# Step one of a Fourier convolution in four 64 by 64 tiles, with kv and the two intermediates stored in another order

## The chip, the cores and the metric

The kernel runs on one core of a Trainium2 chip. The metric is the device time of one execution in microseconds. The five engines of the core have short names here: PE (TensorE matmul, with PEld for its weight loads), DVE (VectorE), ACT (ScalarE), POOL (GpSimd) and SP (SyncE, whose queue issues most DMAs).

## The reference

The inputs are 2048 tokens by 640 channels in float32.

```python
def _A_ref(q, k, v, shift_k, ssm_k, ssm_D):          # per channel
    k_shift = sum over t<4 of k_pad[:, t:t+S] * shift_k[:, 3-t]
    kv = k_shift * v
    y = irfft(rfft(pad(kv, 2S)) * rfft(pad(ssm_k, 2S)))[:S] + kv * ssm_D
    return q * y

def _B_ref(x, w1, b1, w2, b2):                       # MLP over the tokens, F = 1728
    u = gelu(layernorm(x)^T @ w1 + b1)
    return (u @ w2 + b2)^T

sa, ca, ga, sb, cb, gb = split(silu(c) @ w_mod)
x = q
h = layernorm(x) * (1 + ca) + sa
x = x + ga * _A_ref(h, k, v, shift_k, ssm_k, ssm_D)
h = layernorm(x) * (1 + cb) + sb
x = x + gb * _B_ref(h, w1, b1, w2, b2)
```

## The kernel before

The first 350 us of the execution are the long convolution, the rest is the token MLP. The change lies in the first part alone.

The convolution goes through the channels in five chunks of 128 (`NC`, the loop `for c in range(NC)`). Within a chunk the causal convolution of length 2048 is done as a Fourier transform of size 64 by 32 on TensorE. A token index is split into n1 (64 values, on the partitions) and n2 (32 values, free), a frequency into k1 (64) and k2 (32). The two halves of 64 channels of a chunk lie on the lower and the upper 64 partitions (h). A channel within the half is a pair member c or e (2) and an index i (32).

The stages of a chunk, with their names and lines in the profile:

- kv (`kv_ops`, all on L59): four taps multiplied and added, then times v, written into X. DVE does it, but for one of the four groups of the first two chunks, which POOL does. X holds n2 outside and the 64 channels inside. The kv of the next chunk is spread between DVE's other work by `fill` and `dv`, and each group's end issues the loads of a later chunk on SP.
- `perm` (L159): ACT copies the filter from KSR into P in the order (i, n2, e).
- `step1` (L212, evacuation L214): the transform over n1. Side 0 is kv, side 1 the filter. A side has four tiles t of eight indices i. For each i, two matmuls (real and imaginary part, ri) take the data as weights (128 partitions by 64) and the constant F1 as moving operand with 128 columns, block diagonal over the two halves h. Each result occupies 64 partitions and 128 columns of a two-bank PSUM tile, and ACT copies a tile of 1024 elements to Z.
- `f2` (L227): the transform over n2, eight groups g of eight k1. W2 is the weights, Z is the moving operand, 64 columns: both sides, with the 32 indices. ACT copies the filter's spectrum out (L231), DVE multiplies twice into P (L59, `mul`), and POOL adds into Y (L59, `add`; DVE in the last chunk). P has two halves, used in turn.
- `i2` (L256, evacuation L259): the inverse over k2, from Y into T2 in two rounds r, on 32-row tiles. Each round takes two PSUM tiles and four evacuations of 512 elements.
- `i1` (L272): the inverse over k1, in two halves, on tiles of 64 rows and 64 columns: V1 is the weights and T2 the moving operand. Then `gate` multiplies on DVE and adds on POOL.

Z occupies `T_z`, 8192 elements of each partition, side 0 in the lower 4096 and side 1 in the upper 4096. T2 lies over side 1's half. The order of the work is written out by hand: in a chunk c come f2 of c, step one on side 0 of chunk c+1, i2 and i1 of c, and step one on side 1 of c+1. In chunk 0, parts of the modulation (`mod_part`, L343) stand between the tiles of side 0, and the loads of the next w_mod parts, of later k and v and of V1 follow on SP. PSUM tiles come from a ring of three (`psum()`), in turn for all of these stages.

The lines that matter most of what the change rewrites:

```python
Z = T_z.rearrange("p (s t a k e) -> p s t a k e", s=2, t=4, a=8, e=2)
T2 = T_z[:, 4096:8192].rearrange("p (a m e) -> p a m e", a=32, e=2)
```

## Time and profile before

| | |
|---|---|
| median of 3 runs | 771.51 us (770.37 to 774.67) |
| the profiled execution's own time | 767.61 us |
| its span | 765.8 us |
| mean granted TensorE clock | 0.935 |
| PE busy | 665.1 us (87%) |
| DVE busy | 507.1 us (66%) |
| ACT busy | 292.2 us (38%) |
| POOL busy | 177.8 us (23%), all in the first half |

A group row of the profile reads: line, engine, operation, output from input by the program's names, shapes and count, then busy time in us and mean duration of one in ns, then the idle time of the engine just before these instructions and what ended it. Busy times of PE are counted once where matmuls run at the same time on different tiles of the array, while the mean duration is that of one instruction from start to end. So busy time over count tells how often one is finished, and the mean does not. A row of the timeline reads: start, length, engine, line, what it does and how many instructions are merged in it, and in brackets the idle time before it with its releaser. The `L59` lines are the helper through which all tensor-tensor operations go.

### The profile page before, as it was taken

The page shows a single profiled execution, that of the slowest core. Times are in us where ns is not written, and L with a number is a line of the kernel's source. Part 1 is how long each engine was busy: PE and PEld are TensorE (multiplying, and loading weights), DVE is VectorE, ACT ScalarE, POOL GpSimd, SP SyncE. Part 2 cuts the span into 40 slices and gives each one's busy share as a digit, 9 for nine tenths or more (in the row PEclk, how much of TensorE's full clock was granted, in tenths as well). Part 3 has the DMA queues.
Part 4 walks back from the last instruction along what each step waited for, and adds up shares of the span by engine and source line. Part 5 has one row for each costly group of instructions (what it writes and reads, how often), then busy time and mean ns, then how long its engine had stood idle before and what let it go on. Part 6 is the DMA issues. An engine that isn't in the chain of part 4 may idle for free.

```text
span 765.8 us, 20747 instructions
## 1 busy us (share of the span) xinstructions
PE 665.1 (87%) x9117; PEld 641.5 (84%) x9117; DVE 507.1 (66%) x883; ACT 292.2 (38%) x424; POOL 177.8 (23%) x173
## 2 busy tenths in 40 slices
PE   0597948698997989974599999999999989999997
PEld 0597747597997989863599999999999989999997
DVE  4668569974874853958899331312358958888887
ACT  0342324334534544643566622312224323332322
POOL 2268013732842832903253000000000000000000
PEclk9999969888988988976689999999999999999999
DMA  9988886216215024395000244253334262555420
GB/s 169 268 219 250 223 209 140 63 44 119 71 30 112 5 57 135 130 219 111 2 1 1 56 89 77 56 105 61 81 110 141 66 183 86 157 165 156 118 84 35
DMA packets 172425, 84.26 MB, mean 110 GB/s; under 512 B 88959, under 2 KB 164910, under 8 KB 172334
## 3 DMA queue, kind: packets, MB, share of 16 engines
q1 hardware_dynamic: 168110, 81.88, 43.3%
q10 hardware_dynamic: 4224, 1.05, 0.8%
q8 instruction: 71, 1.16, 0.6%
q14 instruction: 20, 0.16, 0.1%
HBM read 72.43 MB, written 10.49 MB: 108 GB/s over the span
## 4 chain that ended last, share of the span: by engine, by line
PE 57%; DVE 20%; DMA 5%; ACT 5%; issue 4%; POOL 4%; SPq 3%; ACTq 0%; DVEq 0%; POOLq 0%
PE pst L420 25%; PE pst L227 8%; PE pst L212 8%; PE pst L909 6%; DVE m_w L59 4%; PE pst L272 4%; PE pst L256 4%; DVE m_x L59 3%; POOL y L59 2%; ACT m_w L822 2%; DVE sm L519 2%; PE pst L834 2%; DMA p<-in_B_w_dram 1%; ACT z L259 1%; DVE m_v L59 1%
## 5 line engine op out<-in xcount | busy, mean ns | idle before, releaser
L59 POOL TENSOR_TENSOR y<-p 128x256 f32<-128x256 f32 x78 | 103.0, 1404 | 37.2 <-DVE p L59 37.2
L227 PE MATMUL pst<-z,w 128*64 128x64 f32 x2560 | 96.3, 240 | 7.2 <-ACT z L214 6.1
L227 PEld LDWEIGHTS pst<-z,w 128*64 128x64 f32 x2560 | 94.9, 141 | 9.1 <-ACT z L214 7.3
L420 PE MATMUL pst<-r_z,wb 128*128 128x320 f32 x504 | 82.8, 321 | 16.1 <-ACT r_z L653 10.6
L420 PEld LDWEIGHTS pst<-r_z,wb 128*128 128x128 f32 x504 | 79.1, 198 | 18.0 <-ACT r_z L653 11.8
L214 ACT ACTIVATE z<-pst 128x1024 f32<-128x1024 f32 x40 | 46.4, 1159 | 69.5 <-PE pst L212 69.5
L59 DVE TENSOR_TENSOR p<-pst,kt 128x512 f32<-128x512 f32 x80 | 52.3, 691 | 30.4 <-ACT kt L231 24.3
L256 PEld LDWEIGHTS pst<-v,y 32*128 32x128 f32 x1280 | 46.1, 220 | 7.6 <-ACT z L259 4.6
L256 PE MATMUL pst<-v,y 32*128 32x64 f32 x1280 | 48.0, 307 | 4.7 <-ACT z L259 4.0
L420 PE MATMUL pst<-h_x,wb 128*128 128x320 f32 x336 | 51.1, 309 | 0.0
L420 PEld LDWEIGHTS pst<-h_x,wb 128*128 128x128 f32 x336 | 49.7, 188 | 0.0
L212 PEld LDWEIGHTS pst<-v,x 128*64 128x64 f32 x640 | 44.7, 219 | 5.7 <-POOL y L59 3.0
L212 PE MATMUL pst<-v,x 128*64 128x128 f32 x640 | 45.8, 309 | 3.4 <-DVE x L59 3.4
L231 ACT ACTIVATE kt<-pst 128x512 f32<-128x512 f32 x40 | 25.1, 628 | 55.1 <-PE pst L227 27.3
L834 PE MATMUL pst<-r_z,m_w 128*128 128x320 f32 x222 | 42.8, 312 | 2.0 <-DVE m_w L59 1.4
L59 DVE TENSOR_TENSOR wb<-x,wb 128x1024 fp32r<-128x1024 f32 (+1 forms) x32 | 36.8, 1188 | 11.4 <-ACT wb L409 11.3
L272 PEld LDWEIGHTS pst<-z,v 64*64 64x64 f32 x1280 | 28.8, 186 | 18.1 <-ACT z L259 9.8
L272 PE MATMUL pst<-z,v 64*64 64x64 f32 x1280 | 29.7, 270 | 16.0 <-ACT z L259 8.6
L714 ACT ACTIVATE pst<-pst,sm 128x640 f32<-128x640 f32 x14 | 10.7, 767 | 85.9 <-PE pst L420 85.9
L212 PE MATMUL pst<-v,p 128*64 128x128 f32 x640 | 36.2, 273 | 4.1 <-ACT p L159 1.9
L212 PEld LDWEIGHTS pst<-v,p 128*64 128x64 f32 x640 | 35.0, 137 | 4.6 <-ACT p L159 2.1
L420 PE MATMUL pst<-h_a,wb 128*128 128x320 f32 x252 | 38.8, 309 | 0.0
(209 smaller groups left out, 1281.8 us busy)
## 6 DMA issues: line engine op xcount, KB each, us to landing
x<-in_B_w_dram SPq DMA_DIRECT2D x24, 512.0 KB
m_v<-in_B_w_dram SPq DMA_DIRECT2D x15, 384.0 KB
x<-in_B_w_dram SPq DMA_DIRECT2D x14, 384.0 KB
in<-in_A_k_dram SPq DMA_DIRECT2D x40, 128.0 KB
aux<-in_A_ssm_k_dram SPq DMA_DIRECT2D x10, 512.0 KB
m_x<-xs SPq DMA_DIRECT2D x28, 160.0 KB
out_dram<-m_x SPq DMA_DIRECT2D x28, 160.0 KB
w<-in_const_w_dram SPq DMA_DIRECT2D x2, 2048.0 KB
```

What stands on the lines that cost most here:

```text
L59: TT = lambda eng, o, a, b, op: eng.tensor_tensor(o, a, b, op=op)
L212: pe.matmul(ps[64 * ri:64 * ri + 64, o:o + 128], lhs, F1[:, 128 * ri:128 * ri + 128], start=True, stop=True)
L214: act.activation(Z[:, side, t].rearrange("p a k e -> p e a k"), ps.rearrange("p (e a k) -> p e a k", a=8, e=2), AF.Copy)
L227: pe.matmul(ps[64 * h:64 * h + 64, o:o + 64], W2[k1 // 32][:, 2 * (k1 % 32) + ri], rhs, start=True, stop=True)
L231: act.activation(kt.rearrange("p (m i) -> p m i", i=32), pv[:, :, 1], AF.Copy)
L256: pe.matmul(pp[qd // 2][:, o:o + 64], Y[p, ri, i:i + 2].rearrange("p i k -> p (i k)"), V2[p, 64 * ri:64 * ri + 64], start=ri == 0, stop=ri ...
L272: pe.matmul(ps[64 * b:64 * b + 64, 512 * e + 64 * jj:512 * e + 64 * jj + 64], V1[p, ri, n2], T2[p, :, 32 * ri + n2], start=ri == 0, stop=r ...
L420: pe.matmul(ps[0:m, h, 0:320], w_.bitcast(F32R), r_[:, 320 * h:320 * h + 320].bitcast(F32R), start=first and i == 0, stop=last and i == 2)
L519: dve.bn_stats(bst[:, j, h, :], XR(j, 320 * h, 320))
L822: act.activation(W[n][0].bitcast(F32R), a(w_), AF.Copy)
L834: pe.matmul(bank[n], w[:, i].bitcast(F32R), r.bitcast(F32R), start=i == 0 and k == 0, stop=i == 6 and k == 2)
L909: pe.matmul(acc[s][:, h, 0:320], w[:, f_].bitcast(F32R), u[r + h].bitcast(F32R), start=f_ == 0 and k == 0, stop=f_ == NF - 1 and k == 2)
```

## The change

Four things change, and no arithmetic does.

X gets the order of P, (i, n2, c): the last operation of `kv_ops` writes it through `XP`, so that a weight of side 0 lies in a row of 64 elements, and that write steps 64 elements (256 bytes) between successive elements.

Step one runs the two halves h as matmuls of their own: 64 rows, 64 weight columns, 64 moving columns. The four of an index i (h and ri) lie on the four quadrants of the array, and the two h write to different PSUM banks. The number of matmuls doubles from 16 to 32 a tile.

Z becomes (s, k1, h, i): the evacuation writes with a step of 64 elements, and f2's moving operand becomes two runs of 32 successive elements, where it was 32 pairs, 256 elements apart. The last tile of side 1 is evacuated in two instructions, k1 below 32 first. f2's groups 0 to 3 read only k1 below 32.

T2 becomes (m, s), with the 64 values of s in a row: i2's evacuations write with a step of 64 elements, and i1's moving operand is one run of 64, where it was 32 pairs.

The order of the instructions on each engine stays as it was, apart from the doubled matmuls and the split evacuations. The waits of f2's groups are drawn from the new regions.

```diff
-    KSP = P.rearrange("p (i m) -> p i m", i=32)
+    KSP, XP = [t.rearrange("p (i m) -> p i m", i=32) for t in (P, X)]
...
-    Z = T_z.rearrange("p (s t a k e) -> p s t a k e", s=2, t=4, a=8, e=2)
-    T2 = T_z[:, 4096:8192].rearrange("p (a m e) -> p a m e", a=32, e=2)
+    Z = T_z.rearrange("p (s k h i) -> p s k h i", s=2, k=64, h=2)
+    T2 = T_z[:, 4096:8192].rearrange("p (m s) -> p m s", m=64)
...
-        ops.append(lambda: TT(eng, X.rearrange("p (n i) -> p n i", i=64)[:, 8 * g:8 * g + 8], S_,
-                              VX[:, 8 * g:8 * g + 8], ALU.mult))
+        two = lambda t: t.rearrange("p n (c i) -> p n c i", c=2)
+        ops.append(lambda: TT(eng, XP.rearrange("p i (n c) -> p n c i", c=2)[:, 8 * g:8 * g + 8], two(S_),
+                              two(VX[:, 8 * g:8 * g + 8]), ALU.mult))
...
-            lhs = KSP[:, i] if side else X.rearrange("p (m i) -> p i m", i=32)[:, i]
-            o = 512 * (a % 2) + 128 * (a // 2)
-            for ri in range(2):
-                pe.matmul(ps[64 * ri:64 * ri + 64, o:o + 128], lhs, F1[:, 128 * ri:128 * ri + 128], start=True,
-                          stop=True)
-        act.activation(Z[:, side, t].rearrange("p a k e -> p e a k"),
-                       ps.rearrange("p (e a k) -> p e a k", a=8, e=2), AF.Copy)
+            for h in range(2):
+                r = slice(64 * h, 64 * h + 64)
+                for ri in range(2):
+                    pe.matmul(ps[64 * ri:64 * ri + 64, 512 * h + 64 * a:512 * h + 64 * a + 64],
+                              (KSP if side else XP)[r, i], F1[r, 128 * ri + 64 * h:128 * ri + 64 * h + 64], start=True,
+                              stop=True)
+        n = 32 if side and t == 3 else 64
+        for k in range(0, 64, n):
+            act.activation(Z[:, side, k:k + n, :, 8 * t:8 * t + 8].rearrange("p k h i -> p h i k"),
+                           ps.rearrange("p (h a k) -> p h a k", h=2, a=8)[:, :, :, k:k + n], AF.Copy)
...
-                    rhs = bass.AP(tensor=T_z.tensor, offset=T_z.offset + 128 * h + 2 * k1,
-                                  ap=[T_z.ap[0], [256, 32], [1, 2]])
+                    rhs = bass.AP(tensor=T_z.tensor, offset=T_z.offset + 64 * k1 + 32 * h,
+                                  ap=[T_z.ap[0], [4096, 2], [1, 32]])
...
-            act.activation(T2[:, 8 * qd + 4 * r:8 * qd + 4 * r + 4].rearrange("p a m e -> p a e m"),
-                           pp[qd // 2][:, 512 * (qd % 2):512 * (qd % 2) + 512].rearrange("p (a e m) -> p a e m",
-                                                                                         a=4, e=2), AF.Copy)
+            act.activation(T2[:, :, 16 * qd + 8 * r:16 * qd + 8 * r + 8].rearrange("p m s -> p s m"),
+                           pp[qd // 2][:, 512 * (qd % 2):512 * (qd % 2) + 512].rearrange("p (s m) -> p s m", s=8),
+                           AF.Copy)
...
-                                  V1[p, ri, n2], T2[p, :, 32 * ri + n2], start=ri == 0, stop=ri == 1)
+                                  V1[p, ri, n2], T2[p, 32 * ri + n2], start=ri == 0, stop=ri == 1)
```

## The prediction

> **What bounds the kernel now.** I read the page first (span, chain), then the groups kept apart by shape, then the timeline and the table by stage of the first 350 us, where every edit lies.
>
> ```profile
> span 765.8 us, 20747 instructions
> PE 57%; DVE 20%; DMA 5%; ACT 5%; issue 4%; POOL 4%; SPq 3%; ACTq 0%; DVEq 0%; POOLq 0%
> PE pst L420 25%; PE pst L227 8%; PE pst L212 8%; PE pst L909 6%; DVE m_w L59 4%; PE pst L272 4%; PE pst L256 4%; DVE m_x L59 3%; POOL y L59 2%; ACT m_w L822 2%; DVE sm L519 2%; PE pst L834 2%; DMA p<-in_B_w_dram 1%; ACT z L259 1%; DVE m_v L59 1%
> ```
>
> The chain gives step one (L212) 8% of the span, about 61 us, and ACT's evacuations a little over 1%. The sizes behind it (busy total, mean of one, then idle before):
>
> ```profile
> L227 PE MATMUL pst<-z,w 128*64 128x64 f32 x2560 | 96.3, 240 | 7.2 <-ACT z L214 6.1 <-DVE p L59 1.1
> L212 PE MATMUL pst<-v,x 128*64 128x128 f32 x640 | 45.8, 309 | 3.4 <-DVE x L59 3.4
> L212 PE MATMUL pst<-v,p 128*64 128x128 f32 x640 | 36.2, 273 | 4.1 <-ACT p L159 1.9 <-DVE aux L59 1.8 <-issue 0.4
> L272 PE MATMUL pst<-z,v 64*64 64x64 f32 x1280 | 29.7, 270 | 16.0 <-ACT z L259 8.6 <-DMA v<-in_const_v_dram 5.3 <-issue 2.1
> L214 ACT ACTIVATE z<-pst 128x1024 f32<-128x1024 f32 x40 | 46.4, 1159 | 69.5 <-PE pst L212 69.5
> L259 ACT ACTIVATE z<-pst 128x512 f32<-128x512 f32 x40 | 21.4, 629 | 32.9 <-PE pst L256 32.9
> L159 ACT ACTIVATE p<-aux 128x2048 f32<-128x2048 f32 x5 | 10.5, 2097 | 26.0 <-POOL aux L59 26.0
> L409 ACT ACTIVATE wb<-x 128x1024 fp32r<-128x1024 f32 x24 | 24.1, 1050 | 4.7 <-PE pst L420 4.3 <-DMA x<-in_B_w_dram 0.3
> L59 POOL TENSOR_TENSOR y<-p 128x256 f32<-128x256 f32 x78 | 103.0, 1404 | 37.2 <-DVE p L59 37.2
> L59 POOL TENSOR_TENSOR t<-t 128x512 f32<-128x512 f32 x6 | 7.8, 1303 | 0.5
> ```
>
> ACT waits for PE in step one (69.5 us over 40 evacuations): a tile takes PE longer than ACT. The record counts are twice those of the code (16 matmuls a tile, 20 tiles a side, 640 records), so a matmul of step one has two records. Stage by stage (start:end and length; PE, PEld, DVE, ACT, POOL busy with counts; granted clock; DMA share, GB/s):
>
> ```profile
> 239.10:246.20 7.10, 7.10 (x129) 6.90 (x128) 5.35 (x8) 3.39 (x3) 2.38 (x1) 1.00 0.81 157
> 267.10:275.20 8.10, 8.10 (x130) 7.98 (x130) 7.85 (x4) 4.53 (x6) 7.17 (x7) 1.00 0.01 2
> 106.90:110.60 3.70, 3.69 (x136) 3.70 (x137) 1.41 (x5) 0.00 (x0) 0.00 (x0) 0.50 1.20 185
> 111.10:113.30 2.20, 2.20 (x120) 2.08 (x119) 2.13 (x6) 0.16 (x1) 0.97 (x3) 0.87 0.11 18
> 223.60:230.00 6.40, 6.40 (x124) 6.21 (x124) 1.98 (x3) 1.29 (x3) 0.00 (x0) 0.56 0.01 3
> 280.20:285.00 4.80, 4.80 (x124) 4.80 (x124) 0.00 (x0) 0.96 (x2) 0.00 (x0) 0.72 0.38 66
> ```
>
> Row one is step one on the filter (side 1), row two on kv (side 0), both at full clock: 7.1 and 8.1 us for four tiles, 1.78 and 2.03 each. The matmuls are the same; what differs is that X is read as weights in steps of 128 bytes and P in a row. The next two rows are i1, whose matmuls have exactly the new shape (64 rows, 64 columns, N of 64, the same order of the four quadrants). The last two are i2.
>
> **Step one on PE.** i1 took 54 ns a matmul at clock 0.50 (3.69 us over 136 records, two each) and 37 ns at 0.87. Times the clock that is 27 to 32 ns at full speed. A tile becomes 32 such matmuls, 0.9 to 1.0 us; I take 1.02. ACT's evacuation (1.16) then sets the pace, if it keeps that time. What of this reaches the end must be seen in each chunk:
>
> ```profile
> 239.04 7.21 PE L212 MATMUL pst<-v,p 128*64 128x128 f32 x128
> 246.35 1.07 ACT L214 ACTIVATE z<-pst 128x1024 f32<-128x1024 f32 x1 [0.64 <-PE pst L212]
> 247.47 3.77 PE L227 MATMUL pst<-z,w 128*64 128x64 f32 x95 [1.23 <-ACT z L214]
> 153.15 9.41 PE L212 MATMUL pst<-v,x 128*64 128x128 f32 x128
> 152.60 4.19 POOL L59 TENSOR_TENSOR y<-p 128x256 f32<-128x256 f32 x2 [1.17 <-DVE p L59]
> 162.49 4.01 PE L256 MATMUL pst<-v,y 32*128 32x64 f32 x132
> 210.25 8.37 PE L212 MATMUL pst<-v,x 128*64 128x128 f32 x128
> 214.78 3.22 POOL L59 TENSOR_TENSOR y<-p 128x256 f32<-128x256 f32 x1
> 218.55 4.01 PE L256 MATMUL pst<-v,y 32*128 32x64 f32 x132
> 251.60 20.38 POOL L59 TENSOR_TENSOR y<-p 128x256 f32<-128x256 f32 x16 [8.69 <-DVE p L59]
> 267.02 8.25 PE L212 MATMUL pst<-v,x 128*64 128x128 f32 x128 [0.50 <-DVE x L59]
> 275.19 4.01 PE L256 MATMUL pst<-v,y 32*128 32x64 f32 x132
> ```
>
> *Side 1, chunks 1 to 3.* Now 8.43 us from the first matmul to f2 (239.04 to 247.47), and f2 waits for the last evacuation. New: first tile 1.02, 0.1 to signal, three evacuations of 1.15, then only the first half of the last (k1 below 32, 512 elements: 0.63 as L259's), 5.2 in all. Saved 3.2 each, 9.6. The second half runs beside f2's first group.
>
> *Side 0.* i2 follows, and needs two things besides PE: all of Y from POOL, and the second and third tile evacuated, since the ring has three buffers. Chunk 1: evacuations end at 153.15 + 1.2 (9.41 for 8.37 there, a slower clock) + 0.1 + 3 x 1.16 = 157.9, POOL at 156.8; i2 starts at 158.0 for 162.5, 4.5 saved. Chunk 2: POOL ends at 218.0 whatever PE does, so only 0.5 of 8.4 us is saved; POOL's Y is the late one there. Chunk 3: ACT 271.6, POOL 272.0, i2 at 272.1 for 275.2, 3.1 saved. Chunk 4 has no side 0.
>
> ```profile
> 55.38 5.48 POOL L59 TENSOR_TENSOR y<-p 128x256 f32<-128x256 f32 x4
> 78.00 4.28 PE L212 MATMUL pst<-v,x 128*64 128x128 f32 x64
> 106.91 3.91 PE L272 MATMUL pst<-z,v 64*64 64x64 f32 x136 [5.30 <-DMA v<-in_const_v_dram]
> 151.98 1.24 PE L165 MATMUL tap<-rows 2*128 2x256 f32 x2 [5.91 <-DVE x L59]
> ```
>
> *Start and chunk 0.* f2 may start sooner, but Y starts on POOL at 55.4, after POOL's share of kv that its loads hold back: nothing saved. Tiles 2 and 3 of the side 0 at 78.0 stand ahead of the second modulation part, whose end frees the loads behind it on SP, and V1's load last of all, for which i1 waits 5.30 us: 4.28 becomes 2.2, saved 2.1 (0 to 2.5). Side 1 of chunk 0 is worth nothing: chunk 1's f2 ends on DVE (taps wait 5.91 for it).
>
> Together 9.6 + 4.5 + 0.5 + 3.1 + 2.1 = 19.8 us.
>
> **What it costs.** *PE's idle time.* i2's second half runs right after a wait of 1.0 us, at 0.56 in chunk 2 (6.40 us) and at 0.72 in chunk 3 (4.80). In the new chunk 2 PE waits some 3.5 us for POOL ahead of i2: 1.6 lost (0 if the clock holds). *Instructions.* Step one's double, and L272 stood 2.1 us by "issue" in 1280 records; 1280 more, half of them on the path: 1.0 (0 to 2).
>
> *Contiguous moving operand in f2 and i1.* f2 takes 37.6 ns a record (96.3 over 2560). The side-1 step streams 128 columns in 56.6 (36.2 over 640), so 28 would be the floor for 64: up to 0.6 us a group. Only chunk 4's f2 has no POOL or DVE pacing it; at most 4.9 us there, and 1.8 from earlier first groups. i1 reads in the same pairs and is near its floor, so I take 0.
>
> *The strided writes* are the unknown. ACT now writes Z and T2 with 256 bytes between successive elements, DVE and POOL write X so. No row shows a write that steps more than 8 bytes; that one, L159, costs nothing (2097 for 2048 elements against 1050 for 1024). Reads with a long step are slow:
>
> ```profile
> L59 DVE TENSOR_TENSOR y<-p x2: 601/816/1032, 323.2 to 324.2; 128x256 f32<-128x256 f32 x2
> L59 DVE TENSOR_TENSOR x<-tap,in x18: 676/691/702, 15.2 to 266.2; 128x512 f32<-128x512 f32 x18
> L59 DVE TENSOR_TENSOR wb<-x,wb x32: 1082/1219/1227, 324.7 to 602.7; 128x1024 fp32r<-128x1024 f32 x24, 128x896 fp32r<-128x896 f32 x8
> ```
>
> In a row DVE takes 1.03 ns a result and 0.16 us fixed (1219 less 691 over 512). With a 256-byte step in both inputs, at best 601 for 256: 1.71 a result, 0.86 a read. One access each 0.86 ns is what ACT needs at its 1.02 (1047 over 1024), so I take nothing extra for one write per element. The other end adds the full 0.86 per element: 2.04 us for 1024 elements, 1.07 for 512; 0.44 on each X write of DVE; on POOL 2.74 ns a stepped read (1404 over 512) for 1.27 (1303 over 1024), 0.75 an X write. A gain below today's cost I exclude: today's writes step 8 bytes and cost nothing.
>
> [...]
>
> **Sum.** 19.8 less 1.6 and 1.0 is 17.2. The profiled execution took 767.6 (2 outside the span) and becomes 750.4; the median of the three runs, 771.5, stands 3.9 above it, so 754.3, say 754.
>
> **Rivals.** *Strided writes at the far end (slower).* The place is ACT behind i2:
>
> ```profile
> 223.56 6.43 PE L256 MATMUL pst<-v,y 32*128 32x64 f32 x124 [1.00 <-ACT z L259]
> 231.82 5.11 PE L272 MATMUL pst<-z,v 64*64 64x64 f32 x249 [1.82 <-ACT z L259]
> ```
>
> PE waits for two evacuations in the middle and four at the end; 0.44 each is 2.6 a chunk, 10.5 in chunks 1 to 4 and 1.8 in chunk 0. Step one, bound by evacuations of 2.04, keeps 0.1 x 3 on side 1, and 1.9, 0.5, 0.9 and 1.0 on side 0. Chunk 1's four X writes add 1.8, POOL's 0.8. With clock and issue: 12.3 + 2.6 + 2.6 - 4.6 = 12.9 slower, 784. It decides at 0.49 ns an element, an evacuation of 1.66 us. For it: stepped reads do cost. Against: ACT is the slower consumer. *Between:* 1.45 us an evacuation, 0.3 an element, gives back 35% of the 30 us between the ends: 765.
>
> *PE's gaps take the clock down.* With ACT pacing, PE idles in every tile. If each of seven stages is followed by 1.6 of slow clock, 11.2 instead of 1.6 is lost: 764. Against it: f2 runs at 1.00 after a wait of 1.23 today. [...]
>
> That the four tiles don't overlap, so step one gains nothing, the i1 rows speak against; I give it nothing.
>
> **The numbers.** Forecast 0.52; strided writes slow 0.26 (768 to 785); between 0.12; clock 0.10. The low end is 19.8 + 4.9 + 1.8 saved and nothing lost: 745.0, say 744. The high end takes in most of the slow case: 780. The likeliest case's own range is 744 to 760. Half a per cent, 3.9 us, is what a measurement here tells from no change. Faster: 0.52, 0.08 of the clock's and 0.07 of the between case, 0.67. Same: 0.02, 0.05 and 0.04 of the slow case, 0.11. Slower: 0.22.
>
> **What would show it.** Right: L214 at 1.10 to 1.25 us for 1024 elements and L259 near 0.63; L212 some 1.0 us a tile with ACT no longer idle behind it; side 1 to f2 in 5.2; i2 of chunk 2 waiting for POOL. Wrong: L214 above 1.66; PEclk under 0.8 in f2; L212 above 1.5 a tile.

## The result and the profile after

The changed kernel takes 780.7 us (778.4 to 782.8) beside 771.0 for the kernel before, measured with it. The ratio is 1.0115 (1.0067 to 1.0163): slower by over 0.5%, and outside the range of 744 to 780 by 0.7 us. The profiled execution took 782.3 us.

The page of the changed kernel, its span, its granted clock in 40 slices and its chain:

```profile
span 780.5 us, 23315 instructions
PEclk9989867878966886987589999999999999999999
PE 49%; DVE 22%; DMA 8%; issue 8%; ACT 7%; SPq 5%; POOL 0%; ACTq 0%; DVEq 0%
```

PE's share of the chain falls by 8 points, and "issue" and ACT rise from 4 and 5% to 8 and 7. The groups of the first 400 us, kept apart by shape, show three things of different sign:

```profile
L217 ACT ACTIVATE z<-pst 128x1024 f32<-128x1024 f32 x35 | 65.6, 1981 | 54.5 <-PE pst L212 54.5
L262 ACT ACTIVATE z<-pst 128x512 f32<-128x512 f32 x40 | 36.4, 1057 | 30.3 <-PE pst L259 30.3
L59 DVE TENSOR_TENSOR x<-tap,in 128x512 f32<-128x512 f32 x18 | 18.9, 1051 | 2.0 <-PE pst L212 1.5
L212 PE MATMUL pst<-v,x 64*64 64x64 f32 x1280 | 31.3, 277 | 8.6 <-issue 4.7 <-DVE x L59 3.7
L212 PE MATMUL pst<-v,p 64*64 64x64 f32 x1280 | 26.7, 249 | 22.7 <-issue 17.5 <-DVE aux L59 3.6 <-ACT p L158 1.6
L230 PE MATMUL pst<-z,w 128*64 128x64 f32 x2560 | 84.3, 231 | 13.1 <-ACT z L217 6.0 <-DVE p L59 4.8 <-issue 2.2
L59 POOL TENSOR_TENSOR y<-p 128x256 f32<-128x256 f32 x78 | 90.0, 1197 | 51.9 <-DVE p L59 51.9
```

The stepped evacuations cost 0.80 to 0.84 ns an element more (1159 to 1981 for 1024, 629 to 1057 for 512). Step one's matmuls take less of PE (45.8 to 31.3 and 36.2 to 26.7 us busy, part of it at a lower clock), but on side 1 PE now stands 17.5 us for "issue" where it stood 0.4. And f2 takes 12 us less of PE (96.3 to 84.3) and POOL's Y 0.21 us less each (1404 to 1197), for which the forecast took nothing.

The timeline of PE behind chunk 1's inverse shows 6.3 of the 17.5 us:

```profile
177.91 5.34 PE L275 MATMUL pst<-z,v 64*64 64x64 f32 x256 [3.29 <-ACT z L262]
184.95 2.09 PE L212 MATMUL pst<-v,p 64*64 64x64 f32 x127 [1.70 <-issue]
189.47 2.09 PE L212 MATMUL pst<-v,p 64*64 64x64 f32 x128 [2.43 <-issue]
193.74 0.21 PE L212 MATMUL pst<-v,p 64*64 64x64 f32 x1 [2.19 <-issue]
195.13 13.02 PE L230 MATMUL pst<-z,w 128*64 128x64 f32 x384 [1.17 <-ACT z L217]
```

Side 1 is executed in pieces of 127 or 128 records, each 2.09 us long, which start 4.3 to 4.5 us apart. Every matmul record has a weight load beside it, so a piece is 256 instructions. i1 (256 records, 512 instructions) ran just before. The pages list the transfers of instructions by queue, before and after:

```profile
q8 instruction: 71, 1.16, 0.6%
q8 instruction: 81, 1.33, 0.7%
```

The ten transfers more, of 16 KB each, go with 2568 instructions more (20747 and 23315), so one brings some 257, about the 256 of a piece. In the trace of the changed kernel such a transfer lands 1.2 to 1.6 us before the end of every pause for "issue" on side 1 in chunks 1 to 3; in these rows at 183.5, 188.2 and 192.2 us, for pieces that start at 184.95, 189.47 and 193.74. By these times PE waits there for its next block of instructions.

The first row also shows PE waiting 3.29 us for the evacuations of T2 where it waited 1.82. And i2 itself is slower. Chunk 2's two halves, by windows (length; PE, PEld, DVE, ACT, POOL busy with counts; granted clock; DMA share, GB/s):

```profile
223.00:229.00 6.00, 5.36 (x128) 5.36 (x128) 5.69 (x8) 2.53 (x3) 0.19 (x1) 0.70 0.02 5
231.00:238.00 7.00, 6.89 (x124) 6.70 (x124) 0.95 (x2) 1.95 (x3) 0.00 (x0) 0.50 0.01 2
```

The same 124 to 132 records took 4.01 us at clock 1.00 before (first half) and 6.40 at 0.56.

To compare kernels, the table adds up chunks 1 to 3 from PE's timelines, from the start of one stage to that of the next, in us. The last two columns are the whole way from chunk 1's f2 to chunk 4's, and the median time. The kernels from e1 on are described below.

| kernel | f2 to side 0 | side 0 to i2 | i2 to i1 | i1 to side 1 | side 1 to f2 | sum | median |
|---|---|---|---|---|---|---|---|
| before | 67.6 | 25.8 | 37.3 | 20.3 | 25.3 | 176.3 | 771.0 |
| after | 70.3 | 20.2 | 50.8 | 20.1 | 30.7 | 192.1 | 780.7 |
| e1 | 74.7 | 20.5 | 48.6 | 20.9 | 28.6 | 193.4 | 780.7 |
| e2 | 66.4 | 25.2 | 47.6 | 20.4 | 25.9 | 185.5 | 776.1 |
| e3 | 68.7 | 24.3 | 36.3 | 20.0 | 29.4 | 178.6 | 772.4 |
| e5 | 63.5 | 27.1 | 38.9 | 20.2 | 25.8 | 175.6 | 764.9 |
| e7 | 66.4 | 18.1 | 46.6 | 19.9 | 25.9 | 176.8 | 765.7 |
| e0 | 70.5 | 17.9 | 47.3 | 19.8 | 28.8 | 184.3 | 772.5 |
| e8 | 73.1 | 22.5 | 45.7 | 16.1 | 26.3 | 183.7 | 772.3 |
| e11 | 63.7 | 26.4 | 33.0 | 16.1 | 25.9 | 165.2 | 752.9 |
| e12 | 67.6 | 25.0 | 35.3 | 15.7 | 25.3 | 168.9 | 761.6 |
| e14 | 66.2 | 20.8 | 34.9 | 15.4 | 25.9 | 163.2 | 755.9 |

In these three chunks the change gains 5.6 us where side 0 runs and loses 13.5 between i2 and i1, 5.4 on side 1, and 2.7 between f2 and side 0: 15.8 more, where the whole span grew by 14.7. Each row is a single profiled execution, and the runs of one kernel lie up to 11 us apart (e1: 775.0 to 786.0), so a difference of 2 or 3 us in one column may be chance.

### The profile page after: what moved, and what is told of

It is laid out like the page before. It is cut to its first block, busy times and chain, and to the rows that moved or that the text cites. A ratio compares the mean times of both kernels' runs of the same rounds, so it can differ in the third digit from the quotient of the medians.

```text
span 780.5 us, 23315 instructions
## 1 busy us (share of the span) xinstructions
PE 634.9 (81%) x10397; PEld 608.7 (78%) x10397; DVE 509.5 (65%) x883; ACT 333.5 (43%) x429; POOL 166.5 (21%) x173
## 3 DMA queue, kind: packets, MB, share of 16 engines
q10 hardware_dynamic: 4224, 1.05, 0.8%
## 4 chain that ended last, share of the span: by engine, by line
PE 49%; DVE 22%; DMA 8%; issue 8%; ACT 7%; SPq 5%; POOL 0%; ACTq 0%; DVEq 0%
PE pst L423 25%; PE pst L912 6%; PE pst L212 5%; PE pst L259 4%; DVE m_w L59 4%; PE pst L230 4%; PE pst L275 3%; SPq L487 3%; DVE p L59 3%; DVE m_x L59 3%; ACT z L262 2%; ACT z L217 2%; DVE tap L59 2%; PE pst L837 2%; DMA p<-in_B_w_dram 1%
## 5 line engine op out<-in xcount | busy, mean ns | idle before, releaser
L59 POOL TENSOR_TENSOR y<-p 128x256 f32<-128x256 f32 x78 | 90.0, 1197 | 51.9 <-DVE p L59 51.9
L217 ACT ACTIVATE z<-pst 128x1024 f32<-128x1024 f32 (+1 forms) x45 | 75.0, 1776 | 57.4 <-PE pst L212 57.4
L230 PEld LDWEIGHTS pst<-z,w 128*64 128x64 f32 x2560 | 82.4, 146 | 17.4 <-ACT z L217 9.1
L423 PE MATMUL pst<-r_z,wb 128*128 128x320 f32 x504 | 82.8, 321 | 16.1 <-ACT r_z L656 10.6
L230 PE MATMUL pst<-z,w 128*64 128x64 f32 x2560 | 84.3, 231 | 13.1 <-ACT z L217 6.0
L59 DVE TENSOR_TENSOR p<-pst,kt 128x512 f32<-128x512 f32 x80 | 51.6, 680 | 32.5 <-ACT kt L234 30.7
L259 PE MATMUL pst<-v,y 32*128 32x64 f32 x1280 | 53.0, 327 | 10.0 <-ACT z L262 7.4
L259 PEld LDWEIGHTS pst<-v,y 32*128 32x128 f32 x1280 | 50.8, 239 | 13.1 <-ACT z L262 8.1
L262 ACT ACTIVATE z<-pst 128x512 f32<-128x512 f32 x40 | 36.4, 1057 | 30.3 <-PE pst L259 30.3
L212 PE MATMUL pst<-v,p 64*64 64x64 f32 x1280 | 26.7, 249 | 22.7 <-issue 17.5
L275 PE MATMUL pst<-z,v 64*64 64x64 f32 x1280 | 29.7, 275 | 17.5 <-ACT z L262 12.4
L212 PEld LDWEIGHTS pst<-v,p 64*64 64x64 f32 x1280 | 24.9, 162 | 21.9 <-issue 13.8
L59 DVE TENSOR_TENSOR aux<-pst,aux 128x1024 f32<-128x1024 f32 x10 | 12.2, 1221 | 44.1 <-PE pst L275 44.0
L825 ACT ACTIVATE m_w<-m_v 128x896 fp32r<-128x896 f32 x24 | 22.2, 950 | 42.1 <-DVE m_v L59 29.4
```

Of the source, the lines that this page charges most:

```text
L59: TT = lambda eng, o, a, b, op: eng.tensor_tensor(o, a, b, op=op)
L212: pe.matmul(ps[64 * ri:64 * ri + 64, 512 * h + 64 * a:512 * h + 64 * a + 64], (KSP if side else XP)[r, i], F1[r, 128 * ri + 64 * h:128 * r ...
L217: act.activation(Z[:, side, k:k + n, :, 8 * t:8 * t + 8].rearrange("p k h i -> p h i k"), ps.rearrange("p (h a k) -> p h a k", h=2, a=8)[: ...
L230: pe.matmul(ps[64 * h:64 * h + 64, o:o + 64], W2[k1 // 32][:, 2 * (k1 % 32) + ri], rhs, start=True, stop=True)
L259: pe.matmul(pp[qd // 2][:, o:o + 64], Y[p, ri, i:i + 2].rearrange("p i k -> p (i k)"), V2[p, 64 * ri:64 * ri + 64], start=ri == 0, stop=ri ...
L262: act.activation(T2[:, :, 16 * qd + 8 * r:16 * qd + 8 * r + 8].rearrange("p m s -> p s m"), pp[qd // 2][:, 512 * (qd % 2):512 * (qd % 2) + ...
```

## The experiments

Theories: **W**, the stepped writes on ACT are the loss. **I**, small tiles double the instructions, and PE waits for them. **C**, PE's waits bring the granted clock down, so time saved on PE comes back as a slower i2.

Below, Z or T2 "in rows" is the order of the change (PE reads successive elements, ACT writes with a step of 256 bytes), and "in pairs" is the order of before (PE reads two successive elements and then makes a long step, ACT writes with a step of 8 bytes). X "in its new order" is that of the change.

**e1: small tiles, but no stepped evacuation.** Z and T2 in pairs as before, X in its new order.

```diff
-    Z = T_z.rearrange("p (s k h i) -> p s k h i", s=2, k=64, h=2)
-    T2 = T_z[:, 4096:8192].rearrange("p (m s) -> p m s", m=64)
+    Z = T_z.rearrange("p (s t x k e) -> p s t x k e", s=2, t=4, x=8, e=2)
+    T2 = T_z[:, 4096:8192].rearrange("p (a m e) -> p a m e", a=32, e=2)
...
```

> Step one in four tiles as in the change, but Z and T2 in an order that ACT writes in steps of 8 bytes again; X by channel pairs as in the change. Theory W (ACT's writes in steps of 256 bytes cost 0.8 ns an element, and that is the loss): the evacuation is back at 1.16 us for 1024 elements and 0.63 for 512, i2's waits go back to 1.1 and 2.0 us, side 1 to f2 takes 5 to 6 us, and the kernel takes about 757. Theory I (doubling step one's PE instructions makes PE wait for instructions wherever DMAs are busy): the evacuations are as fast, but PE still stands idle by issue in side 1's stage, one step of 4.3 us for each 256 PE instructions, side 1 to f2 takes 10 us or more, and the kernel takes 766 to 772.

Measured: 780.7 us, ratio 1.0128 (1.0084 to 1.0173), as slow as the change and slower than either theory gave. Its groups:

```profile
L217 ACT ACTIVATE z<-pst 128x1024 f32<-128x1024 f32 x35 | 38.0, 1115 | 62.2 <-PE pst L212 62.1
L212 PE MATMUL pst<-v,p 64*64 64x64 f32 x1280 | 25.5, 241 | 23.1 <-issue 17.7 <-DVE aux L59 3.6 <-ACT p L158 1.7
```

The evacuations are back at 1.12 us and the loss stays, so W alone falls. The 17.7 us of "issue" belong to the small tiles, whatever the writes do.

**e2: only the writes.** Step one on 128 rows; Z, T2 and X ordered as in the change.

```diff
+            for ri in range(2):
+                pe.matmul(ps[64 * ri:64 * ri + 64, 128 * a:128 * a + 128], (KSP if side else XP)[:, i],
+                          F1[:, 128 * ri:128 * ri + 128], start=True, stop=True)
...
```

> Step one on 128 rows as before (16 matmuls a tile), with the change's orders of X, Z and T2, so with all its stepped writes. Theory W: L217-type evacuations at 1.97 us and 1.05 us, i2 2.6 us longer in each chunk, four X writes of DVE 0.35 longer in chunk 1, f2 at 33 ns a record instead of 38: 779 to 785. Theory I: side 1 has no issue gaps and takes 8.4 us to f2 as before, so that this one is faster than the change by the gaps, 6 us in each of three chunks less what the tiles gave: 770 to 776.

Measured: 776.1 us, ratio 1.0068 (1.0033 to 1.0102), just above what theory I gave and below W's range. Both causes exist, and do not add up: this kernel loses 5.2 us and e1 9.9 (X's new order is in both), which is more than the 9 or 10 of the whole. The evacuations take 2011 and 1062 ns, side 1 to f2 stays at 25.9, and i2 to i1 goes from 37.3 to 47.6.

**e3: e1 with X in its old order,** so that DVE and POOL write it in a row and side 0's small tiles read their weights in steps of 128 bytes (set against e1; the write of X is as before).

```diff
+    XO = X.rearrange("p (m i) -> p i m", i=32)
-                              (KSP if side else XP)[r, i], F1[r, 128 * ri + 64 * h:128 * ri + 64 * h + 64], start=True,
+                              (KSP if side else XO)[r, i], F1[r, 128 * ri + 64 * h:128 * ri + 64 * h + 64], start=True,
...
```

> As the tiles with writes in pairs, and X too in its old order, so that DVE and POOL write it in a row and PE reads side 0's weights in steps of 128 bytes. If the X write's 0.35 us on DVE lies on chunk 1's path, this is 1 to 2 us faster; if weights in steps hold up the small tiles as they did the large ones (8.1 for 7.1 us a stage), a tile of side 0 takes 1.3 us for 1.0, past ACT's 1.16, and it is 1 to 2 us slower in side 0's stages.

Measured: 772.4 us, ratio 1.0024 (0.9996 to 1.0052), 8 us less than e1 where 1 to 2 either way were expected.

```profile
L212 PE MATMUL pst<-v,x 64*64 64x64 f32 x1280 | 41.4, 300 | 4.2 <-DVE x L59 3.3 <-issue 0.9
```

Stepped weights hold side 0 at 41.4 us of PE instead of 27.2. The slower side 0 gives the faster kernel: i2 to i1 is 36.3 in e3 and 48.6 in e1. That is what pointed to C. X's writes play a part too: f2 to side 0, where they lie, is 6.0 us shorter than in e1 (a write of DVE takes 691 ns here and 1183 there).

**e4: e1 with the stores of the result and the load of a later filter issued behind side 1,** to take DMA traffic out of the pauses.

```diff
-            if c + 2 < NC:
-                load_ks(c + 2)
...
-            spill(c)
-        if cn is not None:
             for t in range(4):
                 step1(1, t)
+            spill(c)
+            if c + 2 < NC:
+                load_ks(c + 2)
```

> As the tiles with writes in pairs, but the spill of x and the load of the chunk after next's filter are issued after side 1's step one, not ahead of it, so that fewer transfers run in that stage (the loads of k and v stay). Theory W: no difference beyond 1 us. Theory I: the issue gaps in side 1's stage shrink from 2.2 to 2.5 us each to under 1.5, and the kernel is 4 to 10 us faster than with the transfers ahead.

Measured: 781.9 us, ratio 1.0142 (1.0101 to 1.0183). "Issue" on side 1 is 17.4 us, so these transfers are not what PE waits for, and the part of theory I that blamed busy DMAs falls. In chunk 1 the pieces start 3.7 and 4.8 us apart, and around the first (179 to 182 us) the DMA engines were busy for only 2% of the time.

**e5: only the spectrum's order.** Z as in the change; step one on 128 rows, X and T2 as before.

```diff
-    Z = T_z.rearrange("p (s t a k e) -> p s t a k e", s=2, t=4, a=8, e=2)
+    Z = T_z.rearrange("p (s k h i) -> p s k h i", s=2, k=64, h=2)
...
-                    rhs = bass.AP(tensor=T_z.tensor, offset=T_z.offset + 128 * h + 2 * k1,
-                                  ap=[T_z.ap[0], [256, 32], [1, 2]])
+                    rhs = bass.AP(tensor=T_z.tensor, offset=T_z.offset + 64 * k1 + 32 * h,
+                                  ap=[T_z.ap[0], [4096, 2], [1, 32]])
...
```

> Only the spectrum's new order (k1 outermost, both sides 32 columns in a row for f2) with step one on 128 rows, kv and the inverse's intermediate as before. Theory W (the stepped writes of the inverse's intermediate are what e2 lost, since they stand between i2 and i1): intervals i2 to i1 in chunks 1 to 3 back at 12 to 13.3 us each (16.5, 14.7, 16.5 in e2), evacuations of step one at 2.0 us, f2's PE time near 79 us and POOL's Y writes near 1.19 us as in e2, so about 5 us gained: 766 us (762 to 769). Rival (the stepped evacuations of step one cost as much as those of the inverse): no gain, 771 to 776 us.

Measured: 764.9 us, ratio 0.9909 (0.9871 to 0.9947): faster than before.

```profile
L227 PE MATMUL pst<-z,w 128*64 128x64 f32 x2560 | 79.6, 225 | 16.8 <-ACT z L214 6.8 <-DVE p L59 6.8 <-issue 3.1
L214 ACT ACTIVATE z<-pst 128x1024 f32<-128x1024 f32 x35 | 67.4, 1985 | 53.0 <-PE pst L210 52.6
L59 POOL TENSOR_TENSOR y<-p 128x256 f32<-128x256 f32 x78 | 90.4, 1198 | 41.8 <-DVE p L59 41.8
```

The stepped evacuations of Z are in it (1985 ns), and nearly all hidden: a tile on 128 rows takes PE 1.8 to 2.1 us, and behind the split last one PE waits 1.4 us ahead of f2 for 1.2 before. The gain is f2's. e2 is this kernel with T2 in rows and X in its new order, so its 11 us more are theirs.

**e0: the change with T2 in pairs** (e5 with both sides in small tiles and X in its new order).

```diff
-    T2 = T_z[:, 4096:8192].rearrange("p (m s) -> p m s", m=64)
+    T2 = T_z[:, 4096:8192].rearrange("p (a m e) -> p a m e", a=32, e=2)
...
```

> The changed kernel with the inverse's intermediate stored in pairs as before. Theory W: the eight evacuations of 512 elements in a chunk go from 1.06 to 0.63 us, two of them stand between i2 and i1, and with what queues behind them i2 to i1 falls from 16.1, 19.2, 15.5 us to 12 to 13 us: about 771 us. Theory C (the granted clock falls because the TensorE waits for the Y of POOL ahead of i2, and i2 then takes longer): the intervals stay at 13.5, 17.3, 17.8 as in e1, 775 to 779 us.

Measured: 772.45 us, ratio 1.0022 (0.9994 to 1.0051). T2 in rows costs the change 8 us, and the time without it is near W's 771 and below the 775 to 779 of C. But i2 to i1 only falls from 50.8 to 47.3, not to the 36 to 39 of W: the rest of the 8 us is spread over the other stages. e0 also differs from e1 in Z's order alone, and takes 8 us less: with small tiles too, Z in rows gains more than its stepped writes cost.

**e7: e0 with side 1 on 128 rows,** side 0 still in small tiles.

```diff
+            if side:
+                for ri in range(2):
+                    pe.matmul(ps[64 * ri:64 * ri + 64, 128 * a:128 * a + 128], KSP[:, i],
+                              F1[:, 128 * ri:128 * ri + 128], start=True, stop=True)
+                continue
...
```

> e0 (the change with the inverse's intermediate in pairs) with step one of side 1 back on 128 rows, side 0 still in tiles of 64 by 64. Theory I (on side 1 the small tiles wait for instructions): idle for issue in side 1 falls from 17.0 us to under 2, step one of side 1 to f2 takes 8.6 us instead of 9.9, 9.0, 10.7, 9.1, and about 4 us go: 768 us (766 to 770). What stays above the 764.9 of e5 would be what the small tiles of side 0 cost through the clock. Rival (the gaps on side 1 are hidden or come back elsewhere): 771 to 774 us.

Measured: 765.7 us, ratio 0.9944 (0.9916 to 0.9973), 6.7 less than e0 and just below what theory I gave. Of this only 3 us are side 1 itself (28.8 to 25.9). Another 4 are f2 behind it (70.5 to 66.4), where the clock is lower behind the pauses on side 1. The first 5 us of f2 in chunks 2 and 3, first e0, then e7:

```profile
188.00:193.00 5.00, 4.82 (x112) 4.82 (x114) 0.71 (x2) 2.38 (x5) 0.00 (x0) 0.66 0.86 220
248.00:253.00 5.00, 4.56 (x86) 4.56 (x88) 0.13 (x1) 2.09 (x4) 0.00 (x0) 0.50 0.00 0
```

```profile
191.00:196.00 5.00, 4.95 (x168) 4.95 (x170) 2.08 (x4) 3.22 (x8) 1.34 (x2) 1.00 0.84 207
245.00:250.00 5.00, 4.61 (x158) 4.61 (x159) 1.77 (x3) 3.22 (x7) 1.01 (x1) 1.00 0.19 53
```

**e10: e1 with eight unread products between i1 and side 1,** that is, matrix products whose result nobody reads. They give the instruction supply 3.7 us in which PE consumes only 32 instructions (16 matmul records and their weight loads).

```diff
+    def warm(ps, n):
+        for _ in range(n):
+            pe.matmul(ps[:, 0:256], F1[:, 0:128], F1, start=True, stop=True)
...
+        if side and t == 0:
+            warm(ps, 8)
```

> e1 with eight unread products of 256 columns (0.57 us each, 4.6 us, 16 instructions) between i1 and step one of side 1, in each chunk. Theory I (the idle stretches in side 1 are the wait for blocks of 256 instructions, of which the sequencer gets one in 3.7 to 4.8 us once i1 has emptied its store): idle for issue in side 1 falls from 17.7 us to under 5, so 18.3 us of products cost only 4 to 6: 784 to 788 us. Rival (small tiles on side 1 stand still for a reason of their own, or because of the transfers of that stretch): idle stays at 15 to 18 us, and the time is 796 to 800 us.

Measured: 784.7 us, ratio 1.0169 (1.0128 to 1.0209). PE in chunk 1, and the group:

```profile
179.66 3.72 PE L206 MATMUL pst<-v 128*128 128x256 f32 x16
183.31 3.26 PE L218 MATMUL pst<-v,p 64*64 64x64 f32 x208
188.17 0.93 PE L218 MATMUL pst<-v,p 64*64 64x64 f32 x48 [1.59 <-issue]
L218 PE MATMUL pst<-v,p 64*64 64x64 f32 x1280 | 22.7, 226 | 10.5 <-issue 9.3 <-DVE aux L59 1.2
```

208 records now run in one piece, and idle time for issue halves, 17.7 to 9.3 us. That is not the "under 5" of theory I, but far from the 15 to 18 of its rival, and the time is inside what I gave it: the products, 18.6 us of PE in all, cost 4.

**e8: e1 with unread products in PE's other waits** (two ahead of the taps, two ahead of i2, one between its halves, three ahead of i1, in chunks 1 to 3).

```diff
         pp = [psum(), psum()]
+        if warm_on[0]:
+            warm(pp[0], 1 if r else 2)
...
```

> e1 (small tiles, pairs in both arrays) with matrix products that nobody reads put where the TensorE waits in chunks 1 to 3: two of 256 columns (0.57 us each) ahead of the taps, two ahead of i2, one between its halves, three ahead of i1. Theory C (the clock falls because the TensorE waits): granted clock in i2 back at 0.9 or more in both halves, i2 to i1 from 13.5, 17.3, 17.8 to about 12 us each, and 770 to 774 us. Rival (i2 is slow in e1 for another reason): clock and intervals stay, and the time is 781 to 786 us, the part of the products that no wait hides added.

Measured: 772.3 us, ratio 1.0022 (0.9993 to 1.0051), 8.4 us less for more work. In chunk 1 it went as C said: both halves of i2 take 3.8 us at clock 1.00, and i2 to i1 10.9 instead of 13.5. In chunks 2 and 3 it did not: 16.3 and 18.5, at 0.50. There the small tiles of side 0, now at full clock, ran into a pause for instructions of 1.4 and 1.5 us ahead of i2 that no product of mine filled. That looks like I feeding C, but chunk 1 had such a pause too, of 1.50 us, and kept its clock. e8 alone does not settle C.

**e11: e5 with the same products** (eight or three ahead of the taps, two between i2's halves, three ahead of i1).

```diff
+            warm(pw, (8 if c == 1 else 3))
...
+            warm(pp[0], 2 if r else 0)
...
+            ps = i1(half, 3 if c and cn is not None and half == 0 else 0)
```

> e5 (only the spectrum's order changed, 764.9 us) with unread products of 256 columns (0.57 us each) in the waits of chunks 1 to 3: eight (chunk 1) or three ahead of the taps, two between the halves of i2, three ahead of i1. Theory C (a wait of about 1 us between the halves of i2 brings the granted clock down some us later): the second half of i2 goes from 6.6, 4.7, 7.0 to 3.8 us, i1 from 6.5, 5.1, 6.2 to about 3.8, and the time to 755 us (752 to 758). Rival (the clock falls for another reason): the halves stay and the time is 765 to 768 us.

Measured: 752.9 us, ratio 0.9788 (0.9755 to 0.9821), the fastest kernel here. Chunk 1's inverse in e5, and the window of its second half:

```profile
164.01 4.01 PE L256 MATMUL pst<-v,y 32*128 32x64 f32 x132
169.01 6.63 PE L256 MATMUL pst<-v,y 32*128 32x64 f32 x124 [0.99 <-ACT z L259]
177.46 6.54 PE L272 MATMUL pst<-z,v 64*64 64x64 f32 x256 [1.82 <-ACT z L259]
170.00:175.00 5.00, 5.00 (x101) 5.00 (x98) 0.00 (x0) 0.00 (x0) 0.00 (x0) 0.50 0.00 0
```

The same in e11:

```profile
160.75 3.87 PE L264 MATMUL pst<-v,y 32*128 32x64 f32 x128
164.55 1.13 PE L206 MATMUL pst<-v 128*128 128x256 f32 x4
165.61 3.96 PE L264 MATMUL pst<-v,y 32*128 32x64 f32 x128
171.65 3.60 PE L281 MATMUL pst<-z,v 64*64 64x64 f32 x229 [0.59 <-ACT z L267]
166.00:169.00 3.00, 3.00 (x116) 3.00 (x114) 0.00 (x0) 0.75 (x2) 0.00 (x0) 1.00 0.03 8
```

A wait of 0.99 us is followed by half the clock. With products in that wait the second half takes 3.96 us instead of 6.63 and i1, to the start of side 1, 5.2 instead of 6.8. That is C: the two kernels differ in the unread products alone.

Which waits have this effect can be read from the clock itself. It changes only at borders that lie 3.41 us apart: in all sixteen traces every stretch at one clock, but the last, which the end cuts off, lasts a whole multiple of that. Call the time between two borders a slot. In before, chunk 2, these are the slot that holds the wait of 1.00 us between i2's halves, the three slots at half clock behind it, and the next slot:

```profile
220.91:224.32 3.41, 2.41 (x84) 2.27 (x80) 3.17 (x6) 1.93 (x4) 0.00 (x0) 1.00 0.02 5
224.32:234.56 10.24, 8.42 (x210) 8.23 (x207) 1.29 (x2) 4.31 (x6) 0.00 (x0) 0.50 0.01 2
234.56:237.97 3.41, 2.37 (x157) 2.29 (x152) 2.69 (x4) 0.00 (x0) 1.36 (x1) 1.00 0.95 154
```

The halvings follow the idle time within one slot. In e3's chunk 1 a border lies in the middle of the same wait, and the second half of i2 keeps its speed:

```profile
167.57 3.79 PE L259 MATMUL pst<-v,y 32*128 32x64 f32 x124 [1.01 <-ACT z L262]
```

Take the 122 slots at full clock, between 60 and 367 us of all traces, in which over nine tenths of PE's records are i2's. All 42 with over 0.6 us of idle time were followed by half the clock, and none of the 64 with under 0.38. Slots of f2 alone kept their clock with up to 1.9 us (1.93 in e0). So C holds for i2 above all, and whether one wait there costs anything also depends on where a border falls. Why i2 is the more sensitive stage, no run shows.

**e12: the kernel before with such products.**

```diff
+            warm(pw, (8 if c == 1 else 1))
...
+            warm(pp[0], 2 if r else 0)
...
+            ps = i1(half, 3 if c and cn is not None and half == 0 else 0)
```

> The kernel before with the same unread products: eight (chunk 1) or one ahead of the taps, two between the halves of i2, three ahead of i1. Theory C: the second half of i2 in chunk 2 goes from 6.4 to 3.8 us and those of the other two alike, 4 to 8 us in all: 764 us (762 to 767). Rival: 771 to 774 us.

Measured: 761.6 us, ratio 0.9898 (0.9865 to 0.9932), just below the range of C. So the clock was costing the kernel before too.

**m1: the steps by themselves,** as unread work in the kernel before, between the two sides of the first chunk.

```diff
+    rows = lambda st: bass.AP(tensor=MB.tensor, offset=MB.offset, ap=[MB.ap[0], [64 * st, max(1, 8 // st)], [1, min(st, 8)], [st, 64]])
+    act.activation(rows(64), src(mps, 64), AF.Copy)
...
+    TT(dve, rows(64), src(MW, 64), src(MW[:, 512:1024], 64), ALU.mult)
...
+    for j in range(32):
+        pe.matmul(mp2[64 * (j % 2):64 * (j % 2) + 64, 64 * (j // 4):64 * (j // 4) + 64], MW[:, 1024:1088], cols_(64), start=True, stop=True)
...
```

> The kernel before with unread work between the two sides of the first chunk's step one: writes of 512 elements with steps of 1, 2, 4, 8, 16, 32 and 64 elements by ACT, DVE and POOL, and 32 products of 64 columns each whose moving operand, and then whose weights, are read with those steps. Theory W: ACT needs 0.63 us up to some step and 1.06 us at 64, with the rise at one step and not in proportion; DVE rises likewise by 0.35 us, POOL not at all. For the TensorE: the moving operand in a row is faster than pairs at a step by 15 to 20 percent (f2 took 96 us before and 80 with rows), and weights at a step of 64 elements are slower than weights in a row. Rival (the cost is one of the collision of the write with f2's reading): ACT and DVE show no rise here.

ACT, 512 elements at steps of 1, 2, 4 and 64 elements, and PE, 32 products with the moving operand at steps of 1, 2, 4 and 64 and (L527) in pairs:

```profile
50.10 0.60 ACT L490 ACTIVATE z<-pst 128x512 f32<-128x512 f32 x1 [10.30 <-PE pst L484]
50.73 0.66 ACT L491 ACTIVATE z<-pst 128x512 f32<-128x512 f32 x1
51.41 1.13 ACT L492 ACTIVATE z<-pst 128x512 f32<-128x512 f32 x1
...
56.03 1.10 ACT L496 ACTIVATE z<-pst 128x512 f32<-128x512 f32 x1
49.99 2.09 PE L513 MATMUL pst<-w 128*64 128x64 f32 x64
51.91 2.05 PE L515 MATMUL pst<-w 128*64 128x64 f32 x64
53.79 3.87 PE L517 MATMUL pst<-w 128*64 128x64 f32 x64
...
68.82 4.88 PE L525 MATMUL pst<-w 128*64 128x64 f32 x64
73.51 2.58 PE L527 MATMUL pst<-w 128*64 128x64 f32 x64
```

The seven writes of DVE and of POOL (count, then shortest, median and longest in ns):

```profile
L59 DVE TENSOR_TENSOR z<-w x7: 693/1046/1133, 57.2 to 63.1; 128x512 f32<-128x512 f32 x7
L59 POOL TENSOR_TENSOR z<-w x7: 1294/1312/1372, 64.3 to 72.7; 128x512 f32<-128x512 f32 x7
```

The price is a jump between 8 and 16 bytes and not a slope: 0.60 and 0.66 us below, 1.08 to 1.16 at every step from 16 to 256 bytes. DVE does the same (0.69 at the first two steps, 1.04 to 1.13 from the third), POOL does not (1.29 to 1.37 at all). On PE steps up to 8 bytes take 2.1 us, longer ones 3.7 to 4.9, as moving operand and as weights alike; pairs, the old order of Z, take 2.58 for 2.09. So ACT's and DVE's writes and PE's reads all rise between the same two steps.

**e13 and e14: the change, and e7, with unread products.**

```diff
+            warm(pw, (8 if c == 1 else 3))
...
+            warm(pp[0], 3 if r else 2)
...
+            ps = i1(half, 6 if c and cn is not None and half == 0 else 0)
```

(e13; in e14 the 3 between the halves is 2 and the 6 ahead of i1 is 3.)

> The changed kernel with unread products of 256 columns (0.57 us each) in chunks 1 to 3: eight or three ahead of the taps, two ahead of i2, three between its halves, six ahead of i1. If the loss of the stepped writes in the inverse's intermediate is mostly the clock: i2 to i1 falls from 16.1, 19.2, 15.5 to about 13 us each and the time to 766 us (762 to 769). If it is mostly the wait for the evacuations themselves: i2 to i1 stays over 15 us in each and the time is 775 to 781 us.

> e7 (rows in the spectrum, side 0 in small tiles, side 1 on 128 rows, pairs in the inverse) with the same unread products: eight or three ahead of the taps, two ahead of i2, two between its halves, three ahead of i1. If the clock alone took what the small tiles of side 0 gained: s0 to i2 near 7 us, i2 to i1 at 11 to 12 us in all three chunks, and 748 us (745 to 751), below the 752.9 of e11. If the last evacuation of side 0 (1.98 us) and the Y of POOL set the start of i2 anyway: 752 to 757 us.

e13 took 784.2 us (four runs, one at 775.0, the others at 782.8 to 785.9), ratio 1.0137 (1.0081 to 1.0194), outside both expectations; i2 to i1 is 13.3, 20.8 and 14.7. From chunk 1's f2 to chunk 4's its profile takes 185.1 us instead of 192.1, but it reached chunk 1's f2 6.1 us later, at 132.1, in chunk 0 where nothing was added; why is not settled. In chunk 2 both halves of i2 ran at 0.50 behind a pause of 1.30 us for instructions on side 0. How T2's 8 us divide between the wait itself and the clock therefore stays open.

e14 took 755.9 us, ratio 0.9800 (0.9757 to 0.9844). The stages came out much as the first expectation gave them (side 0 to i2 7.0, 7.4 and 6.4; i2 to i1 11.1, 10.9 and 12.9), the time as the second. Side 0 to i2 is 20.8 us for e11's 26.4, yet the time is not shorter than e11's 752.9: 2.5 come back between f2 and side 0, where X's stepped writes lie, 1.9 between i2 and i1, and it starts chunk 1 2.4 later. Small tiles on side 0 gain nothing that can be measured, even at full clock.

## Why the prediction was wrong

Four steps lead from before to after: 771.0; the spectrum's rows alone (e5) 764.9; and side 0 in small tiles with X in its new order (e7) 765.7; and side 1 too (e0) 772.5; and T2 in rows (after) 780.7. So the steps are worth about -6, +1, +7 and +8 us by the medians, and -7, +3, +6 and +7 by the ratios, each taken with its own runs of before; the intervals of e5 and e7 overlap. The forecast had about -10 for side 0 and chunk 0, -10 for side 1, and nothing for the orders of Z and T2.

1. *"I take nothing extra for one write per element."* This step failed. The true price, 0.80 to 0.84 ns an element, is the other end I had named (0.86). The argument that ACT is slow enough to hide one access per element was wrong: in m1 ACT's 512 elements took 0.60 and 0.66 us at steps of 4 and 8 bytes and 1.08 to 1.16 from 16 bytes on, and the row I called a free step (L159) steps by exactly 8. DVE's X write came out at +0.36 us (0.44 given), POOL's at none (1322 before, 1287 after; 0.75 given).

2. *The place of that cost.* The first rival had ACT's size right, and its 784 us are near the result, but it charged step one. e5 shows that Z's stepped writes are nearly hidden on 128 rows and more than repaid in f2, and e0 against e1 that they are repaid with small tiles too. T2's order costs 8 us (after against e0), where 12.3 was given, and X's writes show between f2 and side 0: 2.8 us from e5 to e7, 2.6 given.

3. *Step one on PE.* The rate was right: 2.09 us for 128 records, two tiles, is 1.05 a tile (1.02 forecast). The step that failed is "Instructions ... 1.0 (0 to 2)": 17.5 us of idle time on side 1 in place of 0.4. Side 1 to f2, forecast at 5.2, took 10.2, 10.9 and 9.7 where it had taken 8.4. I had scaled i1's 2.1 us of "issue" by the count, but i1 follows i2, whose 512 instructions spread over 10 to 11 us in before, and side 1 follows i1, whose 512 take 5 to 7 in after. Behind that, 256 more came only every 3.7 to 4.8 us, and small tiles use them in 2.1. That i1 empties a store of instructions, as e10's theory has it, was my assumption: how many PE holds ahead of their use, no run shows.

4. *Side 0.* From the start of side 0 to that of i2 it took 3.2, 2.2 and 0.2 us less (4.5, 0.5, 3.1 forecast): 5.6 of 8.1. In chunk 2 POOL was not late by as much, since its Y was faster. In chunk 3 side 0 ran partly at half clock and paused 0.97 us for instructions.

5. *"1.6 lost (0 if the clock holds)."* Mis-sized, and in the wrong stages. i2 to i1 grew by 13.5 us in chunks 1 to 3. By the rows of PE, 6.5 are longer waits for T2's evacuations, 2.0 are waits for side 0's, and 5.0 are slower matmuls of i2, at a clock down to 0.50. e3 against e1 (12.3 us between i2 and i1 for a slower side 0) points to PE's waits as what lowers it, and e11 shows that filling them brings it back. The clock rival named the mechanism with 11.2 us at seven stages, but gave it 0.10. In i2 over 0.6 us of idle time in a slot of 3.41 was enough, as the 0.56 behind 1.0 us in before's chunk 2 had said already.

6. *Contiguous operand in f2: "I take 0."* It is the one gain that reaches the time. f2 fell to 79.6 us in e5, 0.42 us a group of the 0.6 given as the limit, and POOL's Y fell with it in every kernel with Z in rows (1189 to 1251 ns against 1404 to 1462 with pairs). I had judged that POOL and DVE pace f2 anyway and did not see that POOL would be faster as well.

7. *Chunk 0, 2.1 us.* Not seen: its i1 starts at 107.3 in after and 106.9 before.

Three terms of one sign were mis-sized (T2's writes, side 1's instructions, the clock), and together they outweigh the one on the other side (f2). That the result lies only 0.7 us outside the range is no support for the mechanism: the range's high end takes in most of the case of slow writes, and that case gave the instructions no more than 1.0 us.

## What to carry to other kernels

Where ACT or DVE writes or PE reads on the path, keep the step between successive elements at 8 bytes or less, or let PE read in pairs. In m1 that took ACT 0.60 to 0.66 us and DVE 0.69 for 512 elements, and PE 2.0 to 2.1 us for 32 products (2.58 in pairs). From 16 to 256 bytes the length of the step made little difference to ACT and DVE (1.04 to 1.16 us) and up to a third to PE (3.7 to 4.9 us), so put the long step on an access that another engine hides (Z's writes) and not on one that PE waits for (T2's). Splitting matmuls into small tiles pays only while instructions arrive fast enough: on side 1, behind i1's 512 instructions, the next 256 came every 3.7 to 4.8 us, and small tiles used them in 2.1. And on a part of a kernel where PE waits for a microsecond here and there, look at the granted clock before and after each wait: time saved on PE may only lengthen a wait and halve the clock behind it (e5: 0.50 behind a wait of 0.99 us). Unread products in the wait are a cheap test (e12: 1.0% of the unchanged kernel; with Z in rows, e11: 752.9 us against e5's 764.9).

## What the runs showed of the hardware that was not expected

- The granted clock changes only at borders 3.41 us apart. In i2, a slot with over 0.6 us of idle time was always followed by 0.50, for two to four slots (6.8 to 13.7 us) in chunks 1 to 3 of before and e5; f2 stood up to 1.9 us without it. With the waits filled it is 1.00 from 155 to 316 us (e11).
- PE's instructions come in transfers of 16 KB, some 257 in each (2568 instructions more in ten more of them), and PE went on 1.2 to 1.6 us after one had landed (after, side 1). On side 1 the blocks came 3.7 to 4.8 us apart, and moving the stores and the filter load out of that stretch changed this little (e4: 17.4 for 17.7 us).
- POOL's additions into Y take 1.19 to 1.25 us when PE reads its moving operand in rows and 1.40 to 1.46 when it reads in pairs, with POOL's own operands unchanged. No run here shows the cause.
- The jump of a stepped write is between 8 and 16 bytes on ACT (0.66 and 1.13 us for 512 elements) and DVE (0.69 and 1.13), and POOL shows none (1.29 to 1.37) (m1).
